# Tying each token-row scatter to VectorE's newest attention product, and planning it at a lower rate

## The chip, the core and the metric

One Trainium2 chip, one of its cores. The metric is the device time of one execution, in microseconds (us), from the first to the last instruction of the program with a small fixed part around it. Engines are named as in the profile: PE is the tensor engine (PEld its weight loads), DVE is VectorE, ACT is ScalarE, POOL is GpSimd, SP is SyncE, which here only issues transfers. A DMA that POOL issues (`DMA_INDIRECT`) writes or reads rows at addresses that a table of slots gives.

## The reference

Three stages in float32, one after the other:

```
scores_l = q k^T / 8, kept where |i - j| < 16, else -1e9        # 2 batches, 8 heads, 768 positions, 64 wide
scores_s = q kmax^T / 8 + log(32)                              # kmax: max of k over blocks of 32
a        = softmax([scores_l, scores_s]);  x = a [v, vmean]     # x becomes 1536 tokens x 512
logits   = x w_gate + log1p(exp(x w_noise)) * noise             # 8 experts
top 2 of 8 per token, softmax of the two
out[t]  += weight * relu(x[t] w1[e]) w2[e]                      # 512 -> 1024 -> 512, only the chosen experts
y        = relu(out w_in)^2 w_out                               # 512 -> 2048 -> 512
```

## The kernel before

**Stages.** The attention runs first (about 137 us), then 64 expert units (8 experts of 8 slices of the hidden width), then 48 units of the last layer. A unit is a block of float32 products, each made from three PE passes of split operands (`hi*hi`, `hi*lo`, `lo*hi`, lines 748 to 750). ACT makes the high parts (`wh`, `xh`, `hh`), DVE the low parts (`wl`, `xl`, `hl`).

**Routing.** The 1536 tokens are 12 tiles of 128, called g0 to g11. When a tile's attention is done, PE transposes its columns (`rows`, L397) and DVE scales them into a row tile `xrow` (`x_row`, L401), 128 tokens by 512, of which there are six buffers. When a group of tiles (`GROUPS`: g0 to g5, g6 to g8, g9, g10 and g11) has been routed, `slot_i` holds the two rows of the DRAM buffer `xg` to which each token goes. `scatter(g, k)` (L419) then sends the tile's rows there, once for k = 0 and once for k = 1: 24 scatters, 256 KB each. A scatter is a `memset` of the one-element tile `spacer` (L420) and an indirect DMA (L421), both on POOL. An `xrow` buffer is free for a later tile when both of its scatters have landed.

**Expert 0.** Its rows come in two ways. Rows of g0 to g8 are read back from `xg` by `x_load(0)` (L213, four DMAs on SP, which wait until the 18 scatters of g0 to g8 have landed) and turned by DVE (`x_flip`, L219). Rows of g9 to g11 are picked on PE with one-hot matrices (`pick`, L534; `xpick` is the split row tile, L413 and L415; the products are L470). Both are added up in PSUM (also L470) and split into `xh` and `xl` (L228, L233). The first expert unit needs them. The six scatters of g9 to g11 wait until `x_load(0)` has landed.

**After the attention** POOL fills tables (`tables`, L879 to L892), after all its scatters have landed. One of them, `tb_rc`, is used by DVE at L872; DVE then copies `tb_mp` (L894), and PE needs that copy at L899, between the first and second pair of expert units. From there comes the order of the experts, and with it `x_load(1)` for expert 1.

**What sets the order.** The attention's instructions are placed by the class `Plan`. Each step is a node with an engine, a cost in us, the nodes it depends on and the buffers it takes. The planner goes forward in its own time, starts the ready node with the best rank, and so writes one instruction stream per engine. A scatter is a node on POOL (`"G"`) with cost 1.1 and a further 1.0 until it counts as landed; an `xrow` buffer counts as taken until then, so the cost of a scatter also moves `x_row` nodes of later tiles. On the chip each engine runs its stream in order and waits on semaphores where an operand or a buffer is not ready.

The printed code has `expo`, `e_copy`, `pv` and `x_cols` as the attention steps that feed `x_row`.

Of the kernel before, what the change touches and what calls it, by code (L numbers as in the profile page):

```python
# [7 lines left out]
F32 = mybir.dt.float32  # L8
# [58 lines left out]
GB = 49  # L67
CG = [1 + i * 11 // 5 for i in range(32)]
CB = (3, 2, 2)
TS = (1, 0, 2, 1, 2, 1, 1, 1)  # L70
GT = (0, 1, 3, 4)
G0 = (0, 4, 5, 8, 9)
# [3 lines left out]
class Plan:  # L76
# [6 lines left out]
    def node(self, eng, cost, fn, *deps, take=(), wait=0.0, after=()):  # L83
        n = {"id": len(self.nodes), "eng": eng, "cost": cost, "fn": fn, "deps": deps, "after": after, "take": take,
             "wait": wait, "free": {}}
        self.nodes.append(n)
        return n
# [48 lines left out]
def moe_pipeline_kernel(ctx: ExitStack, tc: tile.TileContext, qT, kT, vW, mk, idm, wg, noise, w1, w2, out):  # L136
    nc = tc.nc
# [19 lines left out]
    spacer = const.tile([1, 1], F32, name="spacer")  # L157
# [77 lines left out]
    def attention(ctx):  # L235
# [34 lines left out]
        node = plan.node  # L270
# [22 lines left out]
        p_t, e_t, et_t, xrow, z_t = {}, {}, {}, {}, {}  # L293
# [47 lines left out]
        def least(s, i, h):  # L341
            t = order[s][2] + i
            m = masks[:, 0 if t == 0 else 2 if t == QT - 1 else 1]
            z = wk.tile([128, NS], F32, name=f"z{h}", bufs=ZB)
            bi = wk.tile([128, 1], F32, name=f"bi{h}", bufs=ZB)
            z_t[s, i, h] = z, bi
            v.tensor_tensor_reduce(out=z, in0=p_t["s", s][:, i, h], in1=m, scale=-0.125, scalar=3.0e38, op0=OP.add,  # L347
                                   op1=OP.min, accum_out=bi)

# [39 lines left out]
        def inverse(g, n):  # L389
            v.tensor_scalar(out=inv[:, g:g + n], in0=sums[:, g:g + n], scalar1=1e-9, scalar2=None, op0=OP.add)  # L390
            v.reciprocal(out=inv[:, g:g + n], in_=inv[:, g:g + n])

        def rows(g):
            b, t = divmod(g, QT)
            p = p_t["r", g] = ps_v.tile([128, 512], F32, name="pv")
            for hp in range(HP):
                nc.tensor.transpose(p[:, hp * 128:(hp + 1) * 128], cols(b, hp, t), ident)  # L397

        def x_row(g):
            xrow[g] = xr_p.tile([128, DM], F32, name="xrow")  # L400
            v.tensor_tensor(out=xrow[g].rearrange("p (h d) -> p h d", d=D), in0=p_t["r", g].rearrange("p (h d) -> p h d", d=D),  # L401
                            in1=inv[:, g, :, None].to_broadcast([128, H, D]), op=OP.mult)

        xpick, room = {}, [ac.tile([128, 4, DM], F32R, name=f"xpick{i}") for i in range((NT - DIRECT + 1) // 2)]
        for g in range(DIRECT, NT):
            i = g - DIRECT
            xpick[g] = [room[i // 2][:, 2 * (i % 2) + j, :] for j in range(2)]

        def x_part(g, k):
            hi, lo = [t.rearrange("p (c a j) -> p c a j", c=4, a=4) for t in xpick[g]]  # L410
            xr = xrow[g].rearrange("p (a c j) -> p c a j", a=4, c=4)
            if k:
                v.tensor_tensor(out=lo, in0=xr, in1=hi.bitcast(F32), op=OP.subtract)  # L413
            else:
                nc.scalar.activation(out=hi, in_=xr, func=AF.Copy)  # L415

        scat = []

        def scatter(g, k):  # L419
            nc.gpsimd.memset(spacer, 0.0)  # L420
            i = nc.gpsimd.indirect_dma_start(out=xg, out_offset=bass.IndirectOffsetOnAxis(ap=slot_i[:, g, k:k + 1], axis=0),  # L421
                                             in_=xrow[g], in_offset=None)
            for j in scat:
                tc.declare_no_dep(i.ins, j.ins, reason="every slot is a row of its own")
            scat.append(i)
# [10 lines left out]
        def gate_copy(g0, n):  # L436
            p_t["l"] = rt.tile([128, 384], F32, name="lt", bufs=1)
            nc.scalar.activation(out=p_t["l"][:, 0:n * 128], in_=p_t["gc", g0][:, 0:n * 128], func=AF.Copy)
# [22 lines left out]
        mp_t, pick, sel = {}, {}, []  # L461
# [14 lines left out]
        def route(g0, n, dep):  # L476
# [6 lines left out]
            def t3(nm):  # L483
                if nm not in st:
                    st[nm] = rt.tile([128, QT, E], U32 if nm == "ix" else F32, name=nm)[:, 0:n, :]
                return st[nm]
# [44 lines left out]

            def one_hot(i):
                pick[g0 + i] = rt.tile([128, CAP], F32R, name="pick", bufs=NT - DIRECT)
                v.tensor_scalar(out=pick[g0 + i], in0=ioc, scalar1=st["mn"][:, i:i + 1], scalar2=None, op0=OP.is_equal)  # L534

            def before():
# [11 lines left out]
            def T(nm):  # L548
# [16 lines left out]
                out=oh, in0=t3("ix")[:, :, 0:2, None].to_broadcast([128, n, 2, E]),  # L565
# [5 lines left out]
            if g0 < DIRECT:  # L571
                out = node("V", 0.06 + 0.02 * n, slot_sum, s0)
            else:
# [4 lines left out]
                out = node("V", 0.07, lambda: v.tensor_copy(out=slot_i[:, g0:g0 + n, :], in_=st["sf"]), s1)  # L578
# [10 lines left out]
        def load(cost, fn, *deps, **kw):  # L589
            return node("D", cost, fn, *deps, wait=LW, **kw)  # L590
# [5 lines left out]
        for u in range(len(heads)):  # L596
# [34 lines left out]
            if u == 1:  # L631
                wvals_n = load(0.9, lambda: (nc.sync.dma_start(out=wg_sb, in_=wg), nc.sync.dma_start(out=nz, in_=noise)),
                               after=[last])
                zero_n = load(2.4, lambda: nc.sync.dma_start(
                    out=xg[0:CAP, :].rearrange("r d -> (r d)").rearrange("(p a c) -> p a c", p=128, a=4),
                    in_=zt[:, None, :].to_broadcast([128, 4, CAP])), set_n, after=[wvals_n])
# [39 lines left out]
        sct, xr_n, lo_n, iv_n, late, gn_l = {}, {}, {}, {}, [], []  # L676
        done = None
        for g0, n in GROUPS:
            for a, m in INVS:
                if g0 <= a < g0 + n:  # L680
                    iv = node("V", 0.14 + 0.07 * m, lambda a=a, m=m: inverse(a, m), *[x for g in range(a, a + m) for x in ex_g[g]])
                    iv_n.update({g: iv for g in range(a, a + m)})
            for g in range(g0, g0 + n):
                rn = node("P", 0.43, lambda g=g: rows(g), *co_g[g], take=("v",), after=[iv_n[g]])
                xr_n[g] = node("V", 0.6, lambda g=g: x_row(g), rn, iv_n[g], take=("xr",))
                plan.free(rn, "v", xr_n[g])
                if g >= DIRECT:
                    hi = node("A", 0.52, lambda g=g: x_part(g, 0), xr_n[g])
                    lo_n[g] = node("V", 0.6, lambda g=g: x_part(g, 1), hi)
            p_t["L", g0] = rt.tile([128, QT, 16], F32, name="L", bufs=len(GROUPS))[:, 0:n, :]  # L690
            gs = []
            for i in range(0, n, 3):
                m = min(3, n - i)
                cg = [c for g in range(g0 + i, g0 + i + m) for c in co_g[g]]
                ivs = [iv_n[g] for g in range(g0 + i, g0 + i + m)]
                if g0 < DIRECT:
                    c0 = node("P", 0.25 * m, lambda a=g0 + i, m=m: gate_cols(a, m), *cg, wvals_n, take=("v",), after=gn_l)
                    c1 = node("A", 0.12 * m, lambda a=g0 + i, m=m: gate_copy(a, m), c0, take=("lt",))
                    plan.free(c0, "v", c1)
                    gn = node("P", 0.11 * m, lambda a=g0 + i, m=m: gate_turn(a, m), c1, take=("v",), after=ivs)  # L700
                    plan.free(c1, "lt", gn)
                    gn_l = [gn]
                else:
                    gn = node("P", 0.43 * m, lambda a=g0 + i, m=m: gate_rows(a, m), *cg, wvals_n, take=("v",), after=ivs)
                w0 = node("V", 0.02 + 0.16 * m, lambda a=g0 + i, m=m: gate_mul(a, m), gn, *ivs, take=("gw",))
                w1 = node("V", 0.02 + 0.16 * m, lambda o=p_t["L", g0][:, i:i + m]: gate_sum(o), w0)
                plan.free(gn, "v", w0)
                plan.free(w0, "gw", w1)
                gs.append(w1)
            gate = node("N", 0.0, lambda: None, *gs, *([done] if done else []))  # L710
            if g0 == DIRECT:
                late = [load(2.4, lambda: x_load(0), *sct.values())]
            done = slot_n = route(g0, n, gate)
            for g in range(g0, g0 + n):
                for k in range(2):
                    sct[g, k] = node("G", 1.1, lambda g=g, k=k: scatter(g, k), slot_n, xr_n[g], zero_n, *late, wait=1.0)
                plan.free(xr_n[g], "xr", sct[g, 0], sct[g, 1], *([lo_n[g]] if g in lo_n else []))
        wl = []
        for _ in range(RBUF):
# [16 lines left out]
    with ExitStack() as actx:  # L736
        attention(actx)
# [77 lines left out]
    def conv_high(i):  # L815
# [3 lines left out]
        hi = c_raw[i][:, :, 1].bitcast(F32)  # L819
        w, r, sg = c_t[i] = [cv.tile([128, 512], d, name=f"c{j}", bufs=CB[j]) for j, d in enumerate((F32, I32, BF))]  # L820
        nc.scalar.activation(out=w, in_=hi, func=AF.Copy, scale=2.0 ** -112)
# [444 lines left out]
    for t in range(NT):  # L1266
        g = GB + GT[t] if t < 4 else n1 + GA + 2 * (t - 4) if t < 8 else n1 + FC2 + GA + 2 * (t - 8)
        for d, fn in zip(G0 if t < 4 else G1, (gather, mix, swap, flip, spread)):
            plan.setdefault(g + d, []).append((fn, t))
    for g in range(n1 + n2 + 1):  # L1270
# [37 lines left out]
        if g == XL1:  # L1308
            x_load(1)
        for _ in range(TS[f] if g > 1 else 1):  # L1310
            next(tsteps, None)
# [60 lines left out]
```

## Time and profile before

| what | value |
|---|---|
| median of 3 runs | 697.51 us (694.77 to 698.63) |
| profiled execution: time / span | 692.52 us / 690.5 us |
| PE busy, share of the span | 640.0 us, 93% |
| DVE, ACT, POOL busy | 440.9 us, 365.7 us, 100.0 us |
| 24 scatters on POOL (L421) | 23.5 us busy, 978 ns each |

The page of the profile sums the span; the timeline of one engine lists its instructions in order of time, with the idle time before each and what ended it; the list of waits sums idle time by who ended it; the table of stretches gives busy time and the granted PE clock stage by stage. Idle time of an engine matters only where the chain to the end runs through it.

### The profile page before, as it was taken

What the parts mean: (1) busy time and instruction counts of PE and PEld (TensorE: products, weight loads), DVE (VectorE), ACT (ScalarE), POOL (GpSimd) and SP (SyncE); (2) the same over time, 40 slices, a digit from 0 to 9 for tenths busy, and PEclk for the clock granted to TensorE, in tenths of its full rate; (3) what the DMA queues carried; (4) which work ended last, traced back from release to release, by engine and by line L of the source; (5) the groups of instructions that cost most, each with busy time, mean ns of one, the idle gap of its engine ahead of it and who ended that gap; (6) DMA issues with size and microseconds to landing.
All of it is one profiled execution on the core that took longest, in us unless ns stands there. A gap on an engine that the chain in (4) does not pass through costs nothing. (4 is left out here: it accounts for less than half of the span.)

```text
span 690.5 us, 11121 instructions
## 1 busy us (share of the span) xinstructions
PE 640.0 (93%) x3928; PEld 572.5 (83%) x3928; DVE 440.9 (64%) x980; ACT 365.7 (53%) x708; POOL 100.0 (14%) x171
## 2 busy tenths in 40 slices
PE   5697866799999999999999999999999999999995
PEld 4576646698999999999999998888878888788884
DVE  5567744686778887767777867666554566554442
ACT  3594551256566656666667666655443544433431
POOL 3000244420101000610004000310042100200002
PEclk9999977799999999999999999999999999999998
DMA  8969435478999998889889898665446544342201
GB/s 205 198 165 211 130 123 166 160 255 288 311 322 289 332 260 292 211 272 265 257 222 391 246 309 244 241 185 159 144 127 207 158 150 122 108 136 91 93 1 64
DMA packets 75740, 139.98 MB, mean 203 GB/s; under 512 B 9041, under 2 KB 44161, under 8 KB 74894
## 3 DMA queue, kind: packets, MB, share of 16 engines
q1 hardware_dynamic: 69566, 116.95, 58.0%
q0 software_dynamic: 6112, 22.25, 8.6%
q8 instruction: 33, 0.54, 0.3%
q14 instruction: 29, 0.24, 0.1%
HBM read 103.27 MB, written 34.88 MB: 200 GB/s over the span
## 5 line engine op out<-in xcount | busy, mean ns | idle before, releaser
L748 PE MATMUL ph<-xh,wh 128*128 128x512 f32 (+8 forms) x448 | 162.8, 363 | 1.8 <-ACT xh L1188 1.8
L750 PE MATMUL ph<-xl,wh 128*128 128x512 f32 (+8 forms) x448 | 162.7, 363 | 1.5 <-DVE xl L1189 1.2
L749 PE MATMUL ph<-xh,wl 128*128 128x512 f32 (+8 forms) x448 | 162.4, 363 | 0.0
L192 DVE TENSOR_TENSOR wl<-wr,wh 128x1024 fp32r<-128x1024 f32 x112 | 136.8, 1221 | 35.2 <-ACT wh L188 32.2
L188 ACT ACTIVATE wh<-wr 128x1024 fp32r<-128x1024 f32 x112 | 117.6, 1050 | 10.3 <-DMA wr<-in_w_dram 7.1
L750 PEld LDWEIGHTS ph<-xl,wh 128*128 128x128 f32 x448 | 84.2, 188 | 10.4 <-DVE xl L1189 2.1
L748 PEld LDWEIGHTS ph<-xh,wh 128*128 128x128 f32 x448 | 84.3, 188 | 10.1 <-ACT xh L1188 2.6
L749 PEld LDWEIGHTS ph<-xh,wl 128*128 128x128 f32 x448 | 84.3, 188 | 7.4
L750 PE MATMUL acc<-hl,wh 128*128 128x416 f32 (+7 forms) x256 | 87.8, 343 | 1.3 <-DVE hl L772 1.3
L749 PE MATMUL acc<-hh,wl 128*128 128x416 f32 (+7 forms) x256 | 87.7, 342 | 0.0
L748 PE MATMUL acc<-hh,wh 128*128 128x416 f32 (+7 forms) x256 | 87.7, 342 | 0.0
L765 ACT ACTIVATE hr<-ph 128x512 f32<-128x512 f32 x48 | 28.7, 598 | 100.3 <-PE ph L750 97.8
L766 DVE SCALAR_TENSOR_TENSOR hg<-ph,hr 128x512 f32<-128x512 f32 x48 | 33.2, 692 | 70.1 <-ACT hr L765 68.2
L749 PE MATMUL acc<-wh,hl 128*128 128x512 f32 x192 | 74.8, 390 | 0.0
L750 PE MATMUL acc<-wl,hh 128*128 128x512 f32 x192 | 74.7, 389 | 0.0
L748 PE MATMUL acc<-wh,hh 128*128 128x512 f32 x192 | 74.7, 389 | 0.0
L771 ACT ACTIVATE hh<-ph 128x416 fp32r<-128x416 f32 (+7 forms) x64 | 32.1, 502 | 80.2 <-PE ph L750 74.8
L772 DVE SCALAR_TENSOR_TENSOR hl<-ph,hh 128x416 fp32r<-128x416 f32 (+7 forms) x64 | 36.5, 570 | 34.5 <-ACT hh L771 32.0
L769 DVE TENSOR_TENSOR hl<-hg,hh 128x512 fp32r<-128x512 f32 x48 | 33.3, 694 | 33.5 <-ACT hh L768 32.8
L768 ACT ACTIVATE hh<-hg 128x512 fp32r<-128x512 f32 x48 | 30.3, 632 | 38.9 <-DVE hg L766 38.0
L354 ACT ACTIVATE es<-z,bi 128x120 f32<-128x120 f32 x96 | 36.6, 383 | 25.9 <-DVE bi L347 25.9
L750 PEld LDWEIGHTS acc<-hl,wh 128*128 128x128 f32 x256 | 48.2, 188 | 1.8 <-DVE hl L772 1.7
(246 smaller groups left out, 915.5 us busy)
## 6 DMA issues: line engine op xcount, KB each, us to landing
wr<-in_w_dram SPq DMA_DIRECT2D x64, 512.0 KB
wr<-w2f SPq DMA_DIRECT2D x48, 512.0 KB
cr<-in_w_dram SPq DMA_DIRECT2D x32, 512.0 KB
w2f<-c SPq DMA_DIRECT2D x32, 256.0 KB
vB<-in_vW_dram SPq DMA_DIRECT2D x8, 576.0 KB
xin<-xg SPq DMA_DIRECT2D x20, 208.0 KB
kB<-in_kT_dram SPq DMA_DIRECT2D x16, 200.0 KB
yg<-ys SPq DMA_DIRECT2D x16, 192.0 KB
```

Source lines behind the costliest of these rows:

```text
L188: nc.scalar.activation(out=hi_t[i], in_=raw_t[i], func=AF.Copy)
L192: nc.vector.tensor_tensor(out=lo_t[i], in0=raw_t.pop(i), in1=hi_t[i].bitcast(F32), op=OP.subtract)
L354: nc.scalar.activation(out=e_t[s][:, i, h], in_=z, func=AF.Exp, bias=bi, scale=-1.0, accum_out=sums[:, b * QT + t0 + i, c:c + 1])
L748: nc.tensor.matmul(out=o, lhsT=wh, rhs=xh, start=first, stop=False)
L749: nc.tensor.matmul(out=o, lhsT=wl, rhs=xh, start=False, stop=False)
L750: nc.tensor.matmul(out=o, lhsT=wh, rhs=xl, start=False, stop=last)
L765: nc.scalar.activation(out=r[:, 0:n], in_=p[:, 0:n], func=AF.Relu)
L766: nc.vector.scalar_tensor_tensor(out=gg[:, 0:n], in0=p[:, 0:n], scalar=0.0, in1=r[:, 0:n], op0=OP.max, op1=OP.mult)
L768: nc.scalar.activation(out=hh[:, 0:n], in_=gg[:, 0:n], func=AF.Copy)
L769: nc.vector.tensor_tensor(out=hl[:, 0:n], in0=gg[:, 0:n], in1=hh[:, 0:n].bitcast(F32), op=OP.subtract)
L771: nc.scalar.activation(out=hh[:, 0:n], in_=p[:, 0:n], func=AF.Relu)
L772: nc.vector.scalar_tensor_tensor(out=hl[:, 0:n], in0=p[:, 0:n], scalar=0.0, in1=hh[:, 0:n].bitcast(F32), op0=OP.max, op1=OP.subtract)
```

## The change

There are two parts. First, a scatter's `memset` of `spacer` becomes a copy from the newest product of DVE: each of `least` (the tile `bi`), `x_row` (`xrow`) and `one_hot` (`pick`) notes its tile in `recent["V"]` when the planner places it, and the scatter copies one element of whatever is noted when the planner places the scatter. On the chip POOL therefore waits, before each scatter, until DVE has come to that instruction. Second, the planner's cost of a scatter goes from 1.1 to `PACE`, 2.5.

```diff
+PACE = 2.5
@@ least
+            recent["V"] = bi[0:1, 0:1]
             v.tensor_tensor_reduce(out=z, in0=p_t["s", s][:, i, h], in1=m, ..., accum_out=bi)
@@ x_row
             xrow[g] = xr_p.tile([128, DM], F32, name="xrow")
+            recent["V"] = xrow[g][0:1, 0:1]
@@ scatter
-        scat = []
+        scat, recent = [], {}
         def scatter(g, k):
-            nc.gpsimd.memset(spacer, 0.0)
+            nc.gpsimd.tensor_copy(out=spacer, in_=recent["V"])
             i = nc.gpsimd.indirect_dma_start(out=xg, ..., in_=xrow[g], in_offset=None)
@@ one_hot
+                recent["V"] = pick[g0 + i][0:1, 0:1].bitcast(F32)
@@ the scatter's node
-                    sct[g, k] = node("G", 1.1, lambda g=g, k=k: scatter(g, k), slot_n, xr_n[g], zero_n, *late, wait=1.0)
+                    sct[g, k] = node("G", PACE, lambda g=g, k=k: scatter(g, k), slot_n, xr_n[g], zero_n, *late, wait=1.0)
```

SP's stream keeps its order. On POOL the scatters keep their order too; what stands before each is new. Before, from the fifth pair on (a number behind a name is its buffer's; `xrow_1348` is tile g4, `xrow_1569` is g5):

```order
L420 MEMSET spacer_83 1x1
L421 DMA xg_74<-xrow_1348,slot_i_79 16384x512
L420 MEMSET spacer_83 1x1
L421 DMA xg_74<-xrow_1348,slot_i_79 16384x512
L420 MEMSET spacer_83 1x1
L421 DMA xg_74<-xrow_1569,slot_i_79 16384x512
```

Now, on POOL, the scatters 12 to 17 of the 18 that `x_load(0)` waits for (here `xrow_1541` is g5, `xrow_1550`, `xrow_1582`, `xrow_1653` are g6, g7, g8, and `xrow_1730`, `xrow_1789`, `xrow_1805` are g9, g10, g11):

```order
L424 COPY spacer_83<-xrow_1789 1x1
L425 DMA xg_74<-xrow_1541,slot_i_79 16384x512
L424 COPY spacer_83<-xrow_1789 1x1
L425 DMA xg_74<-xrow_1550,slot_i_79 16384x512
L424 COPY spacer_83<-xrow_1805 1x1
L425 DMA xg_74<-xrow_1550,slot_i_79 16384x512
L424 COPY spacer_83<-xrow_1805 1x1
L425 DMA xg_74<-xrow_1582,slot_i_79 16384x512
L424 COPY spacer_83<-xrow_1805 1x1
L425 DMA xg_74<-xrow_1582,slot_i_79 16384x512
L424 COPY spacer_83<-xrow_1805 1x1
L425 DMA xg_74<-xrow_1653,slot_i_79 16384x512
```

The scatters 12 and 13 (of g5 and g6) now stand behind DVE's row tile of g10, and the scatters 14 to 24 behind that of g11. Scatters 10 and 11 stand behind g9's. The first nine stand behind `bi` tiles and the row tiles of g6 to g8.

On DVE the row tiles of g10 and g11 move. The end of DVE's attention stream before, from the slots of g10 and g11 on (`pick` is their one-hot matrix, `xtt` the turned rows of `x_load(0)`):

```order
L518 TENSOR_TENSOR sl_1805<-pv_1798,mall_85 128x32
L526 TENSOR_REDUCE sf_1807<-sl_1805 128x4
L530 TENSOR_REDUCE mn_1809<-sf_1807 128x2
L578 CAST slot_i_79<-sf_1807 128x4
L534 TENSOR_SCALAR pick_1812<-ioc_124,mn_1809 128x416
L534 TENSOR_SCALAR pick_1814<-ioc_124,mn_1809 128x416
L219 STREAM_TRANSPOSE xtt_1820<-xin_1767 128x416 x4
```

The same end on DVE now:

```order
L522 TENSOR_TENSOR sl_1778<-pv_1767,mall_85 128x32
L530 TENSOR_REDUCE sf_1780<-sl_1778 128x4
L583 CAST slot_i_79<-sf_1780 128x4
L534 TENSOR_REDUCE mn_1783<-sf_1780 128x2
L539 TENSOR_SCALAR pick_1785<-ioc_124,mn_1783 128x416
L539 TENSOR_SCALAR pick_1787<-ioc_124,mn_1783 128x416
L404 TENSOR_TENSOR xrow_1789<-pv_1717,inv_127 128x512
L416 TENSOR_TENSOR xpick0_134<-xrow_1789,xpick0_134 128x512
L404 TENSOR_TENSOR xrow_1805<-pv_1724,inv_127 128x512
L416 TENSOR_TENSOR xpick1_135<-xrow_1805,xpick1_135 128x512
L220 STREAM_TRANSPOSE xtt_1834<-xin_1827 128x416 x4
```

Two `xrow` and two `xpick` instructions that stood well before the last picks now stand behind them. With six `xrow` buffers, g10's buffer is that of g4 (scatters 9 and 10) and g11's is that of g5 (scatters 11 and 12).

## Rows read from the trace of the kernel before

**Rows 1.** The page: the span, and the granted PE clock in 40 slices.
```profile
span 690.5 us, 11121 instructions
PEclk9999977799999999999999999999999999999998
```
**Rows 2.** Table of stretches: length, busy time by engine (count), clock, DMA share, GB/s.
```profile
75.00:100.00 25.00, 16.27 (x174) 11.94 (x174) 12.67 (x70) 10.32 (x46) 10.75 (x20) 0.78 0.37 131
100.00:125.00 25.00, 18.02 (x166) 16.01 (x162) 12.95 (x50) 7.45 (x29) 9.78 (x19) 0.70 0.53 161
...
200.00:250.00 50.00, 50.00 (x269) 49.82 (x268) 40.22 (x81) 31.26 (x50) 3.30 (x6) 1.00 0.97 301
```
**Rows 3.** List of waits, 80 to 120 us: total, times, longest.
```profile
ACT et L366 <- remote: 8.3, 2, 7.2
PEld ps L336 <- issue: 7.5, 8, 2.6
...
ACT et L366 <- PE ps L336: 5.0, 1, 5.0
```
**Rows 4.** Timeline of POOL: start, length, instruction, idle time before.
```profile
82.11 1.15 POOL L421 DMA_INDIRECT xg<-xrow,slot_i  x1 [74.56 <-DVE bi L347]
...
93.77 0.97 POOL L421 DMA_INDIRECT xg<-xrow,slot_i  x1 [0.22 <-issue]
...
104.68 0.97 POOL L421 DMA_INDIRECT xg<-xrow,slot_i  x1 [9.85 <-DVE sl L518]
...
113.61 0.97 POOL L421 DMA_INDIRECT xg<-xrow,slot_i  x1 [0.23 <-issue]
...
123.47 0.97 POOL L421 DMA_INDIRECT xg<-xrow,slot_i  x1 [8.79 <-DVE L L459]
...
134.34 0.97 POOL L421 DMA_INDIRECT xg<-xrow,slot_i  x1 [0.21 <-issue]
...
139.89 0.23 POOL L892 IOTA tb_rc<- 128x1 int32 x1
```
**Rows 5.** Timeline of PE, 105 to 144 us.
```profile
104.95 0.53 PE L451 MATMUL pv<-wg_sb,xh 128*128 128x32 f32 x4
...
107.64 1.63 PE L377 MATMUL pv<-et,vB 120*64 120x64 f32 x36
...
116.06 1.10 PE L377 MATMUL pv<-et,vB 120*64 120x64 f32 x14 [0.31 <-issue]
...
118.25 1.04 PE L451 MATMUL pv<-wg_sb,xh 128*128 128x32 f32 x4
...
135.92 0.92 PE L470 MATMUL pt<-pick,xpick 128*128 128x416 f32 x4
136.67 0.35 PE L748 MATMUL ph<-xh,wh 128*128 128x416 f32 x1
...
143.57 0.17 PE L899 MATMUL px<-ones,tb_mp 128*24 128x1 bf16 x1
```
**Rows 6.** Timeline of DVE, 124 to 143 us.
```profile
124.09 0.68 DVE L401 TENSOR_TENSOR xrow<-pv,inv 128x512 f32<-128x512 f32 x1
...
125.91 0.68 DVE L413 TENSOR_TENSOR xpick<-xrow,xpick 128x512 fp32r<-128x512 f32 x1
...
130.89 2.08 DVE L219 STREAM_TRANSPOSE xtt<-xin 128x416 f32<-128x416 f32 x4
...
142.20 0.15 DVE L872 TENSOR_SCALAR tb_rc<-tb_rc 128x1 int32<-128x1 int32 x1
```
**Rows 7.** Timeline of SP: the four DMAs of `x_load(0)`.
```profile
116.39 1.89 SPq L213 DMA_DIRECT2D xin<-xg  x4
```
**Rows 8.** DMA traffic from 116 to 124 us in 40 slices of 0.2 us.
```profile
GB/s 0 0 0 0 0 0 8 125 146 241 341 323 346 233 184 172 159 164 184 243 261 213 174 169 179 228 164 256 179 184 246 348 369 410 410 389 430 410 410 430
```
**Rows 9.** List of waits of PE, 137 to 200 us.
```profile
PE acc L750 <- DVE hl L772: 1.3, 1, 1.3
```
**Rows 10.** List of waits of DVE, 137 to 175 us.
```profile
DVE xtt L219 <- DMA xin<-xg: 5.9, 1, 5.9
```

## The prediction

> **What bounds the kernel now.** I read the page first. The span is 690.5 us, and the row of granted clocks is near full but for a dip in its sixth to eighth slices, 86 to 138 us [rows 1]. The table of stretches says the same by stage: from 200 to 250 us PE is busy all the time at full clock, while from 75 to 125 us it is busy 34 of 50 us, at clocks of 0.78 and 0.70 [rows 2]. So the 112 units after 136.67 us, where the first expert product starts [rows 5], are PE's, and what happens before decides when they begin: a microsecond there is a microsecond at the end. The change acts only before that point and on POOL just after it.
>
> Next I read the waits between 80 and 120 us [rows 3], then POOL's timeline [rows 4]. PE's weight loads wait 7.5 us in `L336` for "issue", that is for nothing that the profile shows. ACT waits 5.0 us for PE and 8.3 us for something unnamed. POOL's timeline gives the time of day: ten scatters go out back to back from 82.11 to 94.74 us, eight more from 104.68 to 114.58. PE's timeline puts a stop inside the second train: `L377` runs densely until 109.27, 4.6 us after the train's first scatter, and again from 116.06, 1.5 us after its last one ended [rows 5]. The last scatters, up to 135.31, stop nothing: four passes of `L470` at 135.92 take 0.92 us, as short as any [rows 4, 5].
>
> **What the change can give.** The first train costs ACT 5.0 us for PE and 8.3 - 7.2 = 1.1 us of the unnamed wait, 6.1 us [rows 3]. ACT has the exponentials there and would work on. In the second train, 64 `L377` matmuls run from 107.64 to 117.16 us, 9.5 us; the first 36 take 1.63 us, and at that rate 64 take 2.9 us [rows 5]. That is 6.6 us more. If the first 13 scatters are thin enough to stop nobody, 12.7 us come back; if the stops have another cause, nothing does. I take the whole of it, since the stop of the second train begins and ends with it and the small group stops nothing.
>
> The two `xrow` and two `xpick` instructions that move behind the last picks leave the chain to those picks: 4 x 0.68 = 2.7 us [rows 6]. The transposes begin right behind the picks of g10 and g11, at 130.9 us [rows 6]; I take that for the end of the picks. It becomes 130.9 - 12.7 - 2.7 = 115.5 us. The lower clock there could also lift: four passes of `L451` take 1.04 us at 118.25 against 0.53 at 104.95 [rows 5], so up to 2 us in its 16 passes and, by the same ratio, up to 5 us over all PE work between 88 and 130 us. It may as well stay where it is, because PE still waits for DVE's routing between its pieces. I take 0 and keep 5 for the range.
>
> **What the change costs.** The new order makes one chain of what ran side by side. The scatters 14 to 18 wait for DVE's row tile of g11; that tile needs the buffer of g5, so it waits for scatter 12 to land; scatter 12 waits for the row tile of g10, which now stands behind the last picks. `x_load(0)` waits for scatter 18, and the scatters 19 to 24 wait for `x_load(0)`. With durations from the rows, from the end of the picks:
>
> - row tile of g10, 0.68, as 124.09 [rows 6]; POOL's copy and the gap before a scatter, 0.30, the spacing of 1.28 ((113.61 - 104.68) / 7) less 0.97; scatter 12, 0.97 [rows 4]. Sum 1.95.
> - landing 1.8: scatter 18 ends at 114.58, `x_load(0)` is issued at 116.39 [rows 4, 7]. Sum 3.75.
> - row tile of g11 0.68, gap 0.30, scatters 14 to 18: 4 x 1.28 + 0.97 = 6.09. Sum 10.8.
> - landing 1.8, then the transfer of `x_load(0)`, 6.0: it is issued at 116.39, and the traffic steps up to 410 GB/s at 122.4, when the weights behind it have the queues alone [rows 7, 8]. Sum 18.6.
> - gap 0.30 and six scatters to the start of the last, 5 x 1.28 = 6.4 [rows 4]. Sum 25.3.
> - from the start of the last scatter to the end of the `tb_rc` table, 140.12 - 134.34 = 5.8 (landing, the other tables, a large memset) [rows 4]. Sum 31.1.
>
> Thus the table is done at 115.5 + 31.1 = 146.6 us, and DVE's `L872` runs at 146.7 instead of 142.20 [rows 6]. Before, POOL had finished at 140.12, 2.1 us ahead of need; that cover is gone. DVE runs in order: behind `L872` stand the copy that PE's `L899` needs, before at 143.57 [rows 5], the low parts of the second unit, and the table work that ends in `x_load(1)`. PE already waits for that transfer through DVE, 5.9 us on DVE and 1.3 us on PE [rows 9, 10], so DVE's delay reaches PE whole: 146.7 - 142.2 = 4.5 us.
>
> The other way to the units is shorter. `x_load(0)` lands at 115.5 + 18.6 = 134.1; four transposes, 2.08 [rows 6], and about half a microsecond of the last sum put the first product at 136.7, as before [rows 5]. If PE starts it at half clock after its idle time, the first two units lose some 2 us, and `L899` waits until about 147 us anyway: 136.7 + 2 + (143.57 - 136.67) = 145.6. So this costs nothing beside the table's path. A one-element copy in place of a memset costs nothing either: POOL's own 0.1 us lies in the spacing above. Its reading of `bi` could hold back DVE's next write of that buffer, between 0 and the gap of 0.30 us for each of the four of that kind; I take 0, since that buffer is the fourth to be written. SP's queue holds the weight loads behind `x_load(0)`, issued at 115.5 + 10.8 + 1.8 = 128.1, 12 us later than before; by the code two units' weights are split and a third's loaded by then, so the fourth unit is the first to need a late one. I count 0 for it, at most 1.
>
> **Sum.** -12.7 and -2.7 shorten the chain to the picks, 31.1 us and a semaphore's 0.1 follow where 142.2 - 130.9 = 11.3 followed, so 31.2 - 11.3 - 15.4 = +4.5. On the profiled execution's 692.52 us (the span and 2.0 around it) that is 697.0 us, a factor of 1.0065; on the median of 697.51, which lies 0.7% above that execution, it is 702.0 us.
>
> **Rivals.**
>
> *The stops are not the scatters' doing.* Then PE and ACT stop at the same places, and only 2.7 us come off: the picks end at 128.2, the table at 159.3, DVE is 17.2 us late, 709.7 on the profile and 714.8 us on the median. For it: while a train runs, DMA is only 0.37 to 0.53 busy [rows 2], so the queues are not full. Against it: the second stop keeps its train's times [rows 4, 5]. The Trainium skill, in SBUF — State Buffer, section Who interferes with whom, has the rule that speaks for this rival: a DMA does not contend with a compute engine, and PE and ACT wait on nobody at SBUF. By that rule the time would be 714.8 us; the times of the second train speak against it without showing what the shared thing is. Chance 0.12.
>
> *Faster, by the clock.* If PE keeps its full clock from 88 to 130 us, the 5 us above come off too, and the picks end at 110.5. The table is then ready at 141.6, before DVE wants it, and the price of the chain is gone. The first product comes at 110.5 + 18.6 + 2.6 = 131.7, 5.0 us early; the table's way saves only 0.5 of that, and the end lies between, say 4 us early. That is 688.5, or 693.5 us on the median. It decides from picks at 111.1 on. For it: the clock was low in the slices of the stops [rows 1, 2]. Against it: PE still idles between routing steps. Chance 0.12.
>
> *Half of that clock.* The picks end near 113; +2 us, 699.5 us. Chance 0.28.
>
> *It does not pace what it says.* Scatters 14 to 24 stand behind one product, so five and then six still go back to back. Six beside the first units would stop PE like the second train, 6.6 us for eight, or from the fifth on 1.7 for two each way: 1.7 us, 703.8 us. That lies inside the forecast's own range, 700 to 706, and gets no chance of its own; the forecast has 0.48.
>
> **How the numbers follow.** The likeliest case gives 702.0. The range takes in the faster rival in part and most of the slower one: from 695 to 713. A difference under 0.5%, 3.5 us here, cannot be told from no change. Slower by more holds the first rival and most of the forecast's own range, with a little left to its lower edge: 0.12 + 0.44 = 0.56. Same holds the half clock and that edge: 0.28 + 0.04 = 0.32. Faster: 0.12.
>
> **What would show it.** In the trace after: ACT's and PE's unnamed waits between 85 and 118 us gone or down to 2 us; the last picks at about 115.5; scatter 12 right behind DVE's row tile of g10 and 14 to 18 right behind that of g11; `x_load(0)` issued near 128 instead of 116.39; DVE's `L872` waiting for POOL, at about 146.7, and PE's `L899` right behind. The forecast is wrong if the stops remain, if the picks end before 111, if `L872` does not wait, or if PE makes up the delay at `x_load(1)`.

## The result and the profile after

The changed kernel takes 704.95 us (median of 18 runs, 698.20 to 709.97), the kernel before beside it 697.32 us. The ratio is 1.0100, with a 95% interval of 1.0069 to 1.0130: slower by 5 to 9 us. Run again beside other kernels it took 703.37 us, a ratio of 1.0085 (1.0049 to 1.0122). The span of the profiled execution grew by 699.4 - 690.5 = 8.9 us.

The page of the kernel after, span and granted clock, to be held against [rows 1]:

```profile
span 699.4 us, 11128 instructions
PEclk9898995599999999999999999999999999999999
```

The stretches after, columns as in [rows 2]; the third one is new and comes up below:

```profile
75.00:100.00 25.00, 20.90 (x305) 17.62 (x305) 18.01 (x96) 15.41 (x66) 8.24 (x14) 0.93 0.29 101
100.00:125.00 25.00, 17.30 (x62) 13.15 (x62) 11.94 (x45) 2.59 (x6) 11.92 (x20) 0.55 0.22 85
174.00:178.00 4.00, 4.00 (x14) 3.83 (x14) 3.93 (x10) 3.29 (x6) 0.00 (x0) 0.57 1.04 425
200.00:250.00 50.00, 49.42 (x262) 48.51 (x261) 38.78 (x75) 30.68 (x49) 4.21 (x6) 1.00 0.95 312
```

Between 75 and 100 us PE does 305 matmuls where it did 174, at a clock of 0.93 in place of 0.78. The attention is done sooner. From 100 to 125 us little is left, and the clock falls to 0.55. From 200 to 250 us the units run as before but for 0.6 us.

The list of waits, 80 to 120 us, has no unnamed wait of ACT any more; in the place of the rows of [rows 3] stand these:

```profile
ACT et L368 <- PE pv L379: 2.0, 1, 2.0
...
PEld pv L379 <- issue: 0.8, 3, 0.5
```

POOL's timeline, the second, third, twelfth, fourteenth, eighteenth, nineteenth and last scatter, then the tables; columns as in [rows 4]:

```profile
86.79 0.97 POOL L425 DMA_INDIRECT xg<-xrow,slot_i  x1 [0.53 <-issue]
...
89.72 0.99 POOL L425 DMA_INDIRECT xg<-xrow,slot_i  x1 [0.51 <-issue]
...
115.83 1.41 POOL L425 DMA_INDIRECT xg<-xrow,slot_i  x1 [0.51 <-issue]
...
120.60 1.41 POOL L425 DMA_INDIRECT xg<-xrow,slot_i  x1 [0.51 <-issue]
...
126.29 0.97 POOL L425 DMA_INDIRECT xg<-xrow,slot_i  x1 [0.16 <-issue]
...
136.12 0.98 POOL L425 DMA_INDIRECT xg<-xrow,slot_i  x1 [8.68 <-DMA xin<-xg]
...
142.71 0.97 POOL L425 DMA_INDIRECT xg<-xrow,slot_i  x1 [0.16 <-issue]
145.69 0.15 POOL L884 IOTA tb_iow<- 128x24 f32 x1 [2.01 <-DMA xg<-xrow,slot_i]
...
148.36 0.20 POOL L897 IOTA tb_rc<- 128x1 int32 x1
```

The first six scatters lie 2 to 4 us apart; later ones come in pairs, 1.3 to 1.8 us apart within a pair. The eighteenth, for which `x_load(0)` waits, starts at 126.29 in place of 113.61, and the last at 142.71 in place of 134.34.

DVE's timeline: the last picks, the row tiles of g10 and g11, the turned rows of expert 0, the table, the turned rows of expert 1 (before: [rows 6]):

```profile
113.63 0.78 DVE L539 TENSOR_SCALAR pick<-ioc,mn 128x416 fp32r<-128x416 f32 x2
114.33 0.69 DVE L404 TENSOR_TENSOR xrow<-pv,inv 128x512 f32<-128x512 f32 x1
...
119.09 0.69 DVE L404 TENSOR_TENSOR xrow<-pv,inv 128x512 f32<-128x512 f32 x1 [2.69 <-DMA xg<-xrow,slot_i]
...
135.38 2.09 DVE L220 STREAM_TRANSPOSE xtt<-xin 128x416 f32<-128x416 f32 x4 [14.21 <-DMA xin<-xg]
...
148.59 0.15 DVE L877 TENSOR_SCALAR tb_rc<-tb_rc 128x1 int32<-128x1 int32 x1 [1.58 <-POOL tb_rc L897]
...
170.87 1.17 DVE L220 STREAM_TRANSPOSE xtt<-xin 128x448 f32<-128x448 f32 x2 [7.55 <-DMA xin<-xg]
```

The picks end 16.5 us sooner than before, and DVE then stands still for 14.21 us, until expert 0's rows have landed. SP's timeline, the transfers for expert 0 and for expert 1, shows them issued at 129.05 (before 116.39 [rows 7]) and 164.22 (before 157.25):

```profile
129.05 1.90 SPq L214 DMA_DIRECT2D xin<-xg  x4
...
164.22 1.94 SPq L214 DMA_DIRECT2D xin<-xg  x4
```

PE's timeline, a group of gate products, the first expert product and the table product (before: [rows 5]), and then the list of PE's waits from 137 to 200 us (before: [rows 9]):

```profile
102.80 1.04 PE L455 MATMUL pv<-wg_sb,xh 128*128 128x32 f32 x4
...
140.70 0.67 PE L753 MATMUL ph<-xh,wh 128*128 128x416 f32 x1
...
148.88 0.17 PE L904 MATMUL px<-ones,tb_mp 128*24 128x1 bf16 x1 [0.90 <-DVE tb_mp L899]
```

```profile
PE ps L474 <- DVE xtt L220: 12.0, 1, 12.0
PE acc L755 <- DVE hl L777: 3.1, 1, 3.1
PE px L904 <- DVE tb_mp L899: 0.9, 1, 0.9
```

**Where the 8.9 us lie.** The first expert product starts 140.70 - 136.67 = 4.0 us late. At the table product the delay is 148.88 - 143.57 = 5.3: PE's wait for the table adds 0.9, the first product at half clock (0.67 for 0.35) nearly all of the rest. At `x_load(1)` PE waits 3.1 us where it waited 1.3, 1.8 more. After that wait PE's granted clock is near its lower level from 174 to 178 us, 0.57 in the table of stretches, where the kernel before had 1.00 from 164 us on; 4 us at 0.57 lose 1.7. The sum is 5.3 + 1.8 + 1.7 = 8.8. This is one pair of traces; a second pair, c1 and c2 below, has nearly the same loss in other places.

### The profile page after: what moved, and what is told of

It is laid out like the page before. It is cut to its first block, busy times and chain, and to the rows that moved or that the text cites. A ratio compares the mean times of both kernels' runs of the same rounds, so it can differ in the third digit from the quotient of the medians.

```text
span 699.4 us, 11128 instructions
## 1 busy us (share of the span) xinstructions
PE 645.2 (92%) x3928; PEld 574.1 (82%) x3928; DVE 441.3 (63%) x980; ACT 365.8 (52%) x708; POOL 102.3 (15%) x171
## 5 line engine op out<-in xcount | busy, mean ns | idle before, releaser
L189 ACT ACTIVATE wh<-wr 128x1024 fp32r<-128x1024 f32 x112 | 117.6, 1050 | 12.7 <-DMA wr<-in_w_dram 8.9
```

Source lines behind the costliest of these rows:

```text
L189: nc.scalar.activation(out=hi_t[i], in_=raw_t[i], func=AF.Copy)
```

## The experiments

Twelve runs, in four groups. Kernels of one group (e1 to e4, e5 to e8, c1 to c3, c4) ran on the same chip, each group on another one. In the second and in the last group the kernel before itself took 681.42 us (7 runs) and 679.05 us (17 runs) instead of 697 to 698; why is open, and is taken up below. A ratio holds against the kernel before of its own group; of the second and the last group I use the traces above all.

| run | what | median us | ratio to the kernel before beside it (95%) |
|---|---|---|---|
| e1 | wait, old rate | 695.98 | 0.9948 (0.9909 to 0.9987) |
| e2 | rate, no wait | 699.69 | 1.0014 (0.9980 to 1.0048) |
| e3 | wait for attention steps alone | 697.59 | 0.9986 (0.9942 to 1.0030) |
| e4 | table's column written early | 701.41 | 1.0033 (1.0003 to 1.0063) |
| e5 | 1.64 us by time | 693.53 | 1.0160 (1.0077 to 1.0242), before 681.42 |
| e6 | 2.15 us by time | 697.62 | 1.0265 (1.0185 to 1.0346), before 681.42 |
| e7 | 2.15 us by time, old order | 695.20 | 1.0230 (1.0148 to 1.0312), before 681.42 |
| e8 | no wait for g10, g11, picks | 694.84 | 1.0203 (1.0132 to 1.0274), before 681.42 |
| c1 | the kernel before | 697.26 | 1.0024 (0.9983 to 1.0065) |
| c2 | the changed kernel | 703.37 | 1.0085 (1.0049 to 1.0122) |
| c3 | as e5 | 688.47 | 0.9855 (0.9809 to 0.9901) |
| c4 | 1.46 us by time | 685.17 | 1.0071 (1.0042 to 1.0101), before 679.05 |

**The two parts apart (e1, e2).**

```diff
-PACE = 2.5
+PACE = 1.1
```

> The scatters wait for VectorE's newest product, but the planner counts 1.1 us for each as before (PACE = 1.1), so the order of all other work is that of the kernel before. Theory A (the stops of PE and ACT come from scatters that follow each other every 1.28 us; what delays the changed kernel is the place of scatters 12 to 18 behind the rows of g10 and g11): the named steps lie about 1.1 us apart, so the first train of ten is hardly spaced, its stops stay in part, and the transfer for expert 0 is issued near 116 us as before: 694 to 699 us, the kernel before within 0.5%. Rival B (the wait itself, not the planner's rate, removes the stops): no unnamed wait of PE or ACT between 82 and 116 us, all of 12.7 us come back with the old order: 684 to 690 us.

The spacing is thin: the scatters run in groups of two to four, 1.3 us apart within a group. The list of waits from 80 to 120 us keeps a part of the stops, now more on DVE than on ACT, which has 1.2 and 2.6 us:

```profile
DVE xrow L404 <- remote: 3.6, 1, 3.6
DVE z L349 <- remote: 3.2, 1, 3.2
```

`x_load(0)` is issued at 122.99, not near 116 as theory A had it, but DVE turns its rows at 129.72, right behind the picks and without a wait. So nothing is late: the wait alone is 0.1 to 0.9% faster than the kernel before. That fits theory A in the main; rival B is out.

```diff
-            nc.gpsimd.tensor_copy(out=spacer, in_=recent["V"])
+            nc.gpsimd.memset(spacer, 0.0)
```

> The planner's rate of 2.5 us without the wait: a constant is written to the spacer as before, every other instruction stands where it stands in the changed kernel. Theory A (the loss is the wait's chain behind the rows of g10 and g11): scatters run as soon as their rows are there, back to back again, the stops of 5 to 12 us between 82 and 116 us are back, the transfer for expert 0 is issued near 116 us, the first product comes at 131 to 137 us, and the time is 692 to 698 us, near the kernel before. Rival B (the new order of the other work costs the time): 702 to 706 us, as the changed kernel.

The trains are back, ten scatters from 83.77 and six from 110.10, and so are the stops, in the list of waits from 80 to 120 us:

```profile
ACT et L368 <- remote: 8.1, 2, 5.6
ACT xl L389 <- remote: 7.7, 1, 7.7
```

A lower planned rate spaces nothing on the chip. The time is that of the kernel before within 0.5%, so the new order does not cost the 7 us. But A's bounds were missed, the time by 1.7 us and the first product of 131 to 137 us by 4.9, 141.86: the last picks came at 131.5 and the rows of g10 and g11 behind them. Neither part alone is slower than the kernel before. The changed kernel itself was not run on this chip; e4, which keeps both parts, took 701.41 us here, more than e1 clear of the noise, and more than e2 and e3 with intervals that overlap.

**Is it the chain behind g10 and g11 (e3, e8)?**

```diff
 def x_row(g):
-            recent["V"] = xrow[g][0:1, 0:1]
 def one_hot(i):
-                recent["V"] = pick[g0 + i][0:1, 0:1].bitcast(F32)
```

> The changed kernel, but the newest product is taken from the attention steps alone (the biases of the exponentials), not from the row tiles and picks. Theory A (the chain behind the rows of g10 and g11 makes the transfer for expert 0 late, which makes the first product and the tables late): four scatters are spaced, those from the fifth on run from about 94 us back to back to about 113 us, the transfer for expert 0 is issued at 112 to 116 us instead of 129.05, the first product starts at 124 to 130 us instead of 140.70, the stops come back only beside the last row tiles: 691 to 696 us. Rival B (not that transfer, but the loss of clock and stops in 95 to 115 us decide): the first product stays within 3 us of 140.70 and the time is 701 to 707 us.

`x_load(0)` is issued at 116.11 and the time is 6 to 7 us below the changed kernel's on its chips, as theory A has it, though 1.6 us above A's bounds. But thirteen scatters then run back to back from 92.35 to 108.16, and the stops move there. The list of waits, and below it DVE's row tile of g8, which came at 101.49 in the changed kernel:

```profile
ACT et L368 <- remote: 10.1, 1, 10.1
...
DVE xh L387 <- remote: 6.5, 1, 6.5
```

```profile
111.05 0.68 DVE L403 TENSOR_TENSOR xrow<-pv,inv 128x512 f32<-128x512 f32 x1
```

So the first product came at 134.14, not at 124 to 130: DVE turned expert 0's rows at 128.88 without a wait for the transfer, behind picks that the stops had delayed to 125. A part of what the shorter chain gave was spent on a new train.

```diff
-            recent["V"] = xrow[g][0:1, 0:1]
+            if g < 10:
+                recent["V"] = xrow[g][0:1, 0:1]
 def one_hot(i):
-                recent["V"] = pick[g0 + i][0:1, 0:1].bitcast(F32)
```

> The changed kernel, but the row tiles of g10 and g11 and the picks are not taken as newest product, so that scatters 12 to 24 wait for the row tile of g9 at the latest. Theory A (those two links make the transfer for expert 0 late): scatters 10 to 18 run from about 109 to 120 us, the transfer is issued at 121 to 123 us instead of 129.05 and lands near 128, the first product starts at 132 to 136 us instead of 140.70, the tables as much earlier: 696 to 701 us. Rival B (the table behind the last scatter, or the lower clock of 100 to 140 us, sets the time): first product within 2 us of 140.70, 703 to 706 us.

Here `x_load(0)` is issued at 122.35 and the first product starts at 133.38, both inside A's bounds: the transfer is issued 6.7 us sooner than in the changed kernel and the first product comes 7.3 us sooner. PE still waits 9.4 us for the turned rows (the changed kernel: 12.0), so the transfer still sets it. The median of 694.84 is below both theories' bounds, on the chip with the odd kernel before.

**Is it the table (e4)?**

```diff
 def set_up():
+            nc.gpsimd.iota(part, pattern=[[0, 1]], base=0, channel_multiplier=1, ...)
 def tables():
-        for o, cm in ((pc, 1), (p4, 4), (rc, 1)):
+        for o, cm in ((pc, 1), (p4, 4)):
-        ts(rc, rc, 3, OP.logical_shift_right)
+        ts(rc, part, 3, OP.logical_shift_right)
```

> The changed kernel, with the column of partition numbers for the table tb_rc written by GpSimd in its set-up instead of behind the last scatter, so that VectorE's shift at the start of the tables waits for no scatter. Theory A (the transfer for expert 0 is what is late; the table adds the 0.9 us for which PE waited at its table product, and little behind it): PE's table product comes about 1 us earlier, 703 to 705 us, 0 to 2 us below the changed kernel. Rival B (the way over the last scatter to the table sets the end, as the prediction has it, +4.5 us or more): 699 to 701 us, 4 to 6 us below the changed kernel.

The median is 2.0 us under c2 and 3.5 under the first run of the changed kernel, between the two theories, and the intervals of e4 and c2 overlap: the time settles nothing. The trace shows that the edit did not take the wait away. DVE's first table instruction, L896, waits for the landing of the scatters as POOL's does, and here they landed late. POOL's first table instruction and PE's wait:

```profile
151.96 0.15 POOL L886 IOTA tb_iow<- 128x24 f32 x1 [6.03 <-DMA xg<-xrow,slot_i]
```

```profile
PE px L904 <- DVE tb_rc L879: 3.4, 1, 3.4
```

**Does distance in time do it (e5 to e7, c1 to c4)?** Scatters 1 to 18 are kept apart by POOL's own work, with no wait for DVE: a tile of 128x416 that is zero already is written with zeros once (e5, c3), twice (e6, e7, the latter with `PACE = 1.1`) or by half (c4).

```diff
-            nc.gpsimd.tensor_copy(out=spacer, in_=recent["V"])
+            for _ in range(1 if g < DIRECT else 0):
+                nc.gpsimd.memset(zt, 0.0)
+            nc.gpsimd.memset(spacer, 0.0)
```

> The order of the changed kernel, without the wait for VectorE: before each of scatters 1 to 18 GpSimd writes zeros once to a tile of 128x416 that is zero already (449 ns in the set-up), so that scatters lie about 1.65 us apart by time alone. Theory A (back-to-back scatters stop PE and ACT, spaced ones do not, whatever spaces them; the late transfer for expert 0 is the changed kernel's loss): scatter 18 at about 111 us instead of 126.29, the transfer issued near 112 us, the last pick at 114 to 118 us, the first product at 124 to 130 us instead of 140.70, 689 to 696 us. Rival B (only the wait for VectorE keeps scatters off the steps; a spacing of 1.65 us still stops them): unnamed waits as before the change, first product 135 us or later, 697 us or more.

> As the run before, with the tile written twice, so about 2.1 us between scatters. Theory A: no unnamed waits between 82 and 110 us, scatter 18 at 118 us, the transfer issued near 119 us and landed at 126, the first product at 130 to 133 us, 693 to 699 us; slower than the closer spacing if that one has no stops either. Rival B (the wait, not the distance in time, is what helps): the stops are back, 699 us or more.

> The spacing of 2.1 us by time with the planner's 1.1 us a scatter, so with the order of the kernel before for all other work. Theory A: the stops are gone, so the last pick comes at 118 to 122 us instead of 130.54, the transfer for expert 0 is issued near 119 us and lands near 126, the first product at 131 to 134 us instead of 136.67: 691 to 697 us. Rival (the order of before needs its own waits whatever scatters do): first product at 136 us or later, 697 us or more.

In the traces of e5 and e6 the first product comes at 127.28 and 134.21, inside A's bounds and 1.2 us past them; neither has an unnamed ACT or DVE wait. In e7 it comes at 138.37, later than A allowed, with picks that were done at 117.8; in that the old order's rival is right, though not in the time. But on this chip it is not known whether the kernel before has its stops. So the closest spacing was run again beside both kernels:

> The kernel before once more, unchanged, for a trace on the chip on which the others of this call run; the last four kernels stood against a kernel before that took 681 us where it takes 697 elsewhere. Theory C (on that chip the trains of scatters stop nothing): if this run is near 681 us its trace has no unnamed waits of PE and ACT between 82 and 116 us and the last pick near 118 us; if it is near 697 us the waits are there as in the first trace and the last pick near 130 us. Rival D (that chip is faster elsewhere, in the stages of matmuls after 200 us): near 681 us the waits of 82 to 116 us are there all the same, and the span is shorter behind 200 us.

> The changed kernel once more, unchanged, on the same chip as the others of this call. Theory C: 703 to 706 us, 1.01 of the kernel before, where that takes 697 us; where that takes 681 us, 694 to 705 us, so 1.02 to 1.035, since the stops that the change removes are not there. Rival D: the same ratio of 1.01 on any chip.

> The kernel with one write of a 128x416 tile before each of scatters 1 to 18 and no wait for VectorE, once more, on the same chip as the two others. Theory A (distance in time removes the stops, and the transfer for expert 0 is not late): 691 to 695 us where the kernel before takes 697, a ratio of 0.990 to 0.998, and 8 to 12 us below the changed kernel anywhere. Rival B: no faster than the kernel before, 0.998 or more where that takes 697 us.

On this chip the kernel before takes 697.26 us, and its stops are there. The list of waits of c1, 80 to 120 us:

```profile
ACT et L366 <- remote: 15.4, 3, 7.2
...
PEld ps L336 <- issue: 6.7, 7, 2.5
```

Of c3, with the same eighteen scatters 1.64 us apart instead of 1.28:

```profile
PEld L509 <- issue: 2.3, 1, 2.3
...
ACT xl L389 <- remote: 2.2, 1, 2.2
```

So distance in time is enough, and the wait for DVE is not needed: with 0.36 us more between scatters ACT's unnamed wait is 2.2 us in place of 15.4. The order is not what does it: c3 has the order of the changed kernel, and so has e2, where scatters 1.28 us apart left 15.8, though on another chip. The last picks end at 116.29 (c1: 132.6), `x_load(0)` is issued at 114.83, the first product starts at 125.36 (c1: 140.52). The time is 688.47 us, 1.5% below the kernel before and 15 us below the changed kernel, better than theory A expected. It is the version that beats both, on this chip; on the chip of the second group the same kernel (e5) took 693.53 us and was 1.6% behind the kernel before.

Of 15 us at the first product, 9 reach the end. POOL's timeline of c3, the last scatter and the first table instruction, and PE's waits say where some of the others went:

```profile
128.59 0.96 POOL L427 DMA_INDIRECT xg<-xrow,slot_i  x1 [0.23 <-issue]
135.67 0.15 POOL L886 IOTA tb_iow<- 128x24 f32 x1 [6.12 <-DMA xg<-xrow,slot_i]
```

```profile
PE px L904 <- DVE tb_mp L896: 3.6, 1, 3.6
PE px L906 <- DVE tb_mp L901: 2.5, 1, 2.5
```

The last scatter needs 6.12 us to land, where it needed 1.9 in the first trace of before. SP issues three weight loads of 512 KB at 128.63 to 129.5, at the same moment. In the second trace of the changed kernel (c2) it is the same, scatter 24 at 145.83 and SP's weight load at 145.65:

```profile
145.83 0.97 POOL L425 DMA_INDIRECT xg<-xrow,slot_i  x1 [0.16 <-issue]
152.76 0.15 POOL L884 IOTA tb_iow<- 128x24 f32 x1 [5.97 <-DMA xg<-xrow,slot_i]
```

```profile
PE ps L474 <- DVE xtt L220: 11.9, 1, 11.9
PE px L902 <- DVE tb_mp L894: 3.6, 1, 3.6
PE px L904 <- DVE tb_mp L899: 2.5, 1, 2.5
```

In its first trace the load followed 1.28 us behind the scatter, which landed in 2.01; in c2 PE waits 6.1 us for the table in place of 0.9. In all traces with a weight load less than 1.1 us behind the last scatter, or ahead of it (e4, e5, e8, c2, c3, c4), the landing takes 5.9 to 6.1 us; with 1.28 us or more (first traces of before and after, e1, e6, e7) it takes 1.9 to 2.0, and 2.5 in e2. No run moves the load alone, so that the load is the cause is argued from these traces. I expected a closer spacing to bring the last scatter ahead of the loads:

> As the kernel with one write of a tile between the scatters 1 to 18, but only half of the tile (128x208), so about 1.45 us between scatters in place of 1.65. Theory A (some distance in time over 1.28 us is enough; the table is gated by scatter 24, which lands 6 us after its issue when the three weight loads of 128.6 to 129.9 us stand ahead of it, and 2 us when it stands ahead of them): scatter 18 at about 108 us, the transfer for expert 0 issued near 111 us and landed near 118, scatter 24 issued at 124 to 126 us before any weight load and landed 2 us later, PE's wait at the table product under 2 us in place of 6.1: 683 to 688 us. Rival B (at 1.45 us the stops come back as at 1.28): unnamed waits of 5 us and more between 85 and 108 us, last pick at 122 us or later, 690 to 697 us.

The half tile gives 1.46 us, `x_load(0)` at 110.38, the first product at 121.16, 685.17 us, and ACT and DVE have no unnamed wait. But scatter 24 and the weight load kept their race, at 123.86 and 124.4: both follow the landing of `x_load(0)`, so both moved alike. The load waits for a buffer that DVE's `wl` frees, and it is issued 3.0 to 3.6 us behind the first product in every trace, 3.3 here; the scatter comes 13.5 us after the issue of `x_load(0)`, 13.8 in c3.

```profile
131.32 0.15 POOL L886 IOTA tb_iow<- 128x24 f32 x1 [6.08 <-DMA xg<-xrow,slot_i]
```

This part of theory A fell. Whether 1.46 us is far enough apart is open too, since the kernel before took 679.05 us there.

**The second pair, c1 and c2.** The kernel before itself starts the first product at 136.67 in its first trace and at 140.52 in c1. The picks end 1.6 us later there, and PE adds the turned rows at a lower granted clock, 0.76 from 134.6 to 139.8 us where the first trace has 1.00 from 131 to 136.7. The first trace of before, then c1, then c2:

```profile
131.99 1.56 PE L470 MATMUL ps<-xtt,idz 128*128 128x416 f32 x4
```

```profile
134.61 2.78 PE L470 MATMUL ps<-xtt,idz 128*128 128x416 f32 x4
...
140.52 0.35 PE L748 MATMUL ph<-xh,wh 128*128 128x416 f32 x1
...
147.41 0.17 PE L899 MATMUL px<-ones,tb_mp 128*24 128x1 bf16 x1
```

```profile
142.38 0.67 PE L753 MATMUL ph<-xh,wh 128*128 128x416 f32 x1
...
155.95 0.18 PE L904 MATMUL px<-ones,tb_mp 128*24 128x1 bf16 x1 [2.51 <-DVE tb_mp L899]
```

On this chip the changed kernel's first product is thus only 1.9 us late, and its table product 8.5; the span grows by 8.4 (695.1 to 703.5). Here the loss lies in the table's path, 6.1 us of it in waits for the table, and PE does not wait at `x_load(1)` at all. The 4.0 us at the first product in the first pair are about as large as the 3.9 us between the kernel before's own two traces, so how the loss divides between the two ways is not settled; that the late transfer and the late last scatter feed both is seen in either pair.

**The chips on which the kernel before takes 680 us.** The 12.7 us of stops that the prediction counted, taken from the median of 697.3 us, would leave 684.6, more than the 681 and 679 there, and nine scatters back to back in e8, 107.8 to 119.1 us, left no unnamed wait. So perhaps trains stop nothing on those chips. That is an argument and not shown: no trace of the kernel before is from there, and e8's PE had little to do at that time. Nor is it that such a chip is faster in general: e5 took 693.53 us there, c3, the same kernel, 688.47.

## Why the prediction was right, and where it was not

The forecast of slower, 702.0 us, holds: 704.95. Its mechanism holds as well: the stops go, and a chain behind the row tiles of g10 and g11 costs more than they gave. The size was too small: it had +4.5 us, and there were +7.6 between the medians and +8.9 and +8.4 in the two pairs of traces. That 702.0 lies within 3 us of the time is in part luck, since it counted the table's path alone. In the first pair 3.5 us came at `x_load(1)`, which it did not count; in the second the table was 8.5 us late, because the last scatter took 6 us to land in place of 2. By its steps:

- **The stops, 12.7 us, and the 2.7 us of moved instructions.** Right in their sum. The picks end at 114.41, forecast 115.5. That the close scatters are the cause is shown by e2 (same order without the wait: stops back) and c3 (spaced by time: nearly gone), so the rival that the stops have another cause is out. The Trainium skill, in SBUF — State Buffer, section Who interferes with whom, has it that a DMA never contends with a compute engine and that PE and ACT never wait on anyone. ACT's unnamed waits do change with the distance of the scatters, 15.4 us against 2.2, and no run shows whether they arise at SBUF. How scatters stop the engines stays open.
- **The clock, taken as 0.** It fell instead, from 0.70 to 0.55 in 100 to 125 us, all 16 gate passes at 1.04 us for four, yet the picks came in time. Its loss came elsewhere and was not foreseen: 1.7 us after the stall at `x_load(1)`.
- **The chain of 31.1 us.** The steps are all there, scatter 12 behind g10's row tile, 14 to 18 behind g11's, `x_load(0)` at 129.05 (128.1). It measured 148.56 - 114.41 = 34.2 us. The gap from DVE's row tile to a scatter that waits for it is 0.8 us (a copy of 0.17, 0.51 between copy and scatter, and 0.13 before the copy), not 0.30; a scatter after such a wait took 1.41 us, not 0.97; and from the issue of `x_load(0)` to the next scatter it was 7.1 us, not 6.3.
- **"The other way to the units is shorter ... So this costs nothing beside the table's path."** This step failed. It counted 2.08 and "about half a microsecond" from the transposes to the first product; the trace after has 140.70 - 135.38 = 5.3, and its own rows of before had 136.67 - 130.89 = 5.8 [rows 5, 6]. What it left out are PE's eight products that add the turned rows, and ACT's split of their sum. Read so, the product is forecast at 139.9 and not at 136.7. Both ways were late: in the first trace the table added only 0.9 us to the wait for the transfer, in c2 it added 6.1. That the transfer sets the changed kernel's first product is shown by PE's wait of 12.0 us for the turned rows and by e8. In e3 the picks set it, and in c3 DVE's wait for the transfer is down to 1.1 us.
- **The weight loads, counted 0, at most 1.** Wrong in kind: no unit was late for its weights, but in the traces in which they meet the last scatter its landing takes 4 us longer, and then the table's path costs what the forecast feared and more (c2, 6.1 us).
- **"DVE's delay reaches PE whole" at `x_load(1)`.** It reaches it with interest: that transfer is issued 7.0 us late, PE waits 1.8 us longer and comes out of it near half clock. In c2, where PE had waited at the table, it does not wait there.

The rival that the stops stay is out, and so are both rivals of the clock. That scatters 14 to 24 go back to back is true, and stops nothing that matters: PE has no work from 124.0 to 136.05 us in any case, and beside the last six, 136.12 to 143.7, it has no unnamed wait over 0.5 us.

## What to carry to other kernels

Before you take away a stall, write down what the stalled engine's output waits for next, and time that path from the old trace end to end: here the 5.8 us from transposes to first product stood in the rows and were put at 2.6. Spacing the transfers was worth more here, on the chip of c1 to c3, than ordering them behind another engine, since a wait for the "newest" instruction ties a transfer to whatever happens to be placed there, with all that this waits for. When work moves earlier, look at which transfers now start in the same microsecond.

## What was not expected of the hardware

- Beside ten and eight indirect scatters of 128 rows of 2 KB, 1.28 us apart, ACT has 15.4 us of unnamed waits, and PE's weight loads 6.7 and 6.2 us in two lines (c1), while DMA is only 0.46 to 0.49 busy; with 1.64 us between them ACT has 2.2 us and PE's weight loads 2.3 (c3). Both are from one chip; on the chips where the kernel before takes 680 us it is not shown.
- The last scatter's landing takes 6 us in place of 2 in the six traces in which a plain transfer of 512 KB is issued at most 1.1 us behind it, or just ahead of it.
- PE's clock after a wait does not go by the length of the wait alone. At the same place, `x_load(1)`, waits of 3.1 us (the changed kernel), 1.9 (e3) and 3.2 (e6) were followed by 4 us at a clock of about 0.6; waits of 3.0 us (e1), 1.3 (before) and 1.1 (c1, e2) were followed by full clock.
- The same kernel differs by 16 to 18 us between chips (697 and 681 or 679 us), while a variant of it differs by 5 the other way.
